# Token mixing kept factored: queries, a head matrix and 64-row mixing matmuls in place of a 256x256 mixing matrix

## The chip, the cores and the metric

The kernel runs on one core of a Trainium2 chip. The metric is the device time of one execution in microseconds (us). The kernel before takes 966.49 us, the median of three runs (966.33 to 966.63).

The engines are called as in the profile: PE multiplies matrices (PEld is its loading of weights), DVE, ACT and POOL work element by element, SP issues DMA transfers. Each engine runs its own stream of instructions in order and waits on semaphores for the others. PE writes only to PSUM; DVE and ACT read PSUM and write SBUF.

## What is computed

There are 8 batches of 3200 tokens with 256 columns. The first half is a gated attention over 64-column z, the second a token mixing:

```python
scores = (1/S) * z @ z.T                     # 3200 x 3200 per batch
x      = u * (np.maximum(scores, 0)**2 @ v)  # 3200 x 256
wq, wk = x @ w_q, x @ w_k                    # 3200 x 64
W_tok  = (1/8) * wq @ wk.T                   # 3200 x 3200
out    = np.maximum(W_tok @ x, 0) @ w_out    # 3200 x 256
```

No 3200 x 3200 matrix is needed for the mixing. With the Gram matrix G = xᵀx (256 x 256), W_tok x is, up to the scale, x Wq Wkᵀ G. The kernel before multiplies Wq Wkᵀ G out to one 256 x 256 matrix per batch and applies it to x. The kernel after keeps it in two factors: q = x Wq with 64 columns, and H = Wkᵀ G with 64 rows.

## The kernel before

**Tiles and steps.** The tokens of a batch on the output side are cut into seven groups (512, 512, 512, 512, 384, 384, 384 wide), those on the summed side into 25 tiles of 128. A (batch, group, tile) triple is one unit. The main loop runs over steps of four units (`GRP = 4`), numbered k, 350 in all. A group is 6.25 steps, a batch 43.75.

**One step.** In step k, `scores(k)` makes two PSUM tiles A and B. Each holds two units, computed by a pair of 64-row matmuls, one on partitions 0 to 63 and one on 64 to 127, in two PSUM banks. `first_stage` empties each tile (relu and a factor) to `g`: A always on DVE, B on ACT where k%5 is 1 or 3 and otherwise on DVE. Then come the functions listed for the start of the step (`early`). `second_stage` squares the `g` of the step before: A's on ACT, B's on POOL. Then `outs(k - 4)` multiplies the squared tiles of four steps earlier (`LAG = 4`) with v into a group's accumulator `acc`; that is 16 matmuls of 256 columns, or 12 in a narrow group. When a group's 25th unit is added, `gate` multiplies `acc` with u on DVE into x. At the end of the step come the functions listed in `late`.

All PSUM tiles come from one pool of four buffers, each two banks: `acc` holds one through a group, and scores and all the mixing tiles share the rest.

**The order is written out by hand.** `at_start` and `at_end` put a function at the start or end of a step. `two(k, first, second)` puts a matmul stage at the end of step k and its copy out of PSUM at the start of step k+1. `end_step(b, gi)` is the step in which the last unit of a group passes `outs`. With E for that step of group 6, a batch's mixing stands as follows: `turn_x` (L274) transposes each group of x by DMA into `xT` at the end of the group's own end step; `gram` (L282) makes G at the end of E+2; `mixw` (L300) multiplies G by the matrix `MT` at the end of E+3, in fp32, with `mixw_out` to `jt` on ACT; `mix` (L318) of group 0 comes at the end of E+4, and those of the other groups four steps after an end step of the next batch, one per group. `mix_out` (L332, ACT, relu) follows at the start of the next step and `proj` (L338) at its end. `proj_out` (L354, ACT, in the last batch DVE) and the output DMA come a step later. In the last batch the mixes stand one per step after E+4, with no scores beside them.

`MT` = Wq Wkᵀ is made once, in steps 8 and 10, by `weights_1` (four fp32 transposes, and the cast of w_out to `wo` on DVE) and `weights_2` (two fp32 matmuls).

**Queues.** SP issues in program order the loads of z and u, the spreading of z, the transposes and the output. POOL issues the loads of v (with a cast), one per batch, nine steps after the batch before begins; group 0 of that batch ends at about the tenth step.

Of the kernel before, what the change touches and what calls it, by code (L numbers as in the profile page):

```python
# [9 lines left out]
FP16 = mybir.dt.float16  # L10
FP32 = mybir.dt.float32
# [5 lines left out]
def kernel(  # L17
# [38 lines left out]
    pg = ctx.enter_context(tc.tile_pool(name="pg", bufs=6))  # L56
    pat = ctx.enter_context(tc.tile_pool(name="pat", bufs=12))
    psml = ctx.enter_context(tc.tile_pool(name="psml", bufs=2))
    prt = ctx.enter_context(tc.tile_pool(name="prt", bufs=2))
    pfo = ctx.enter_context(tc.tile_pool(name="pfo", bufs=3))  # L60
    pps = ctx.enter_context(tc.tile_pool(name="pps", bufs=4, space=bass.MemoryType.PSUM))

    def ps_tile(name, dtype=FP32):
        n = W if dtype == FP32 else 2 * W
        return pps.tile([P, 2, n], dtype, tag="ps", name=name)

    ctx.enter_context(tc.manual_schedule())

    zT, vs, us, xs, xTs, jts = {}, {}, {}, {}, {}, {}


    ZCH = [(0, 4), (4, 7), (11, 7), (18, 7)]
# [72 lines left out]
        us[b, gi] = u_sb  # L145


    ident32 = consts.tile([P, P], FP32, tag="ident32", name="ident32")
    ident = consts.tile([P, P], FP16, tag="ident", name="ident")
    wqk32 = consts.tile([P, 2, 2 * dh], FP32, tag="wqk32", name="wqk32")  # L150
    wT = consts.tile([P, 2, D], FP32, tag="wT", name="wT")
    MT = consts.tile([P, ND, D], FP32, tag="MT", name="MT")
    wo32 = consts.tile([P, 2, D], FP32, tag="wo32", name="wo32")
    wo = consts.tile([P, 2, D], FP16, tag="wo", name="wo")

    def load_weights():
        nc.sync.dma_start(out=wqk32[:, :, 0:dh], in_=moe_w_q.rearrange("(c p) h -> p c h", p=P))
        nc.sync.dma_start(out=wqk32[:, :, dh : 2 * dh], in_=moe_w_k.rearrange("(c p) h -> p c h", p=P))
        nc.sync.dma_start(out=wo32[:], in_=moe_w_out.rearrange("(c p) e -> p c e", p=P))

    def weights_1():
        tp = ps_tile("wtp")
        for which in range(2):
            for ac in range(ND):
                nc.tensor.transpose(
                    tp[0:dh, which, ts(ac, P)], wqk32[:, ac, ds(which * dh, dh)], ident32
                )
        nc.scalar.copy(out=wT[0:dh, :, :], in_=tp[0:dh, :, 0:D])
        nc.vector.tensor_copy(out=wo[:], in_=wo32[:])

    def weights_2():
        mp = ps_tile("mtp")
        for cc in range(ND):
            nc.tensor.matmul(  # L174
                out=mp[:, cc, 0:D],
                lhsT=wT[0:dh, 1, ts(cc, P)],
                rhs=wT[0:dh, 0, :],
                start=True,
                stop=True,
            )  # L180
        nc.scalar.copy(out=MT[:], in_=mp[:, :, 0:D])


    tiles = [(b, gi, ti) for b in range(B) for gi in range(NG) for ti in range(NT)]
# [112 lines left out]
        nc.scalar.copy(out=G[:].rearrange("p a d -> p (a d)"), in_=ps[:, 0, :])  # L297
        return G

    def mixw(b, G):  # L300
        ps = ps_tile("jtp")
        for ac in range(ND):
            for cc in range(ND):
                nc.tensor.matmul(  # L304
                    out=ps[:, ac, 0:D],
                    lhsT=MT[:, cc, ts(ac, P)],
                    rhs=G[:, cc, :],
                    start=(cc == 0),
                    stop=(cc == ND - 1),
                )  # L310
        return ps

    def mixw_out(b, ps):
        jt = psml.tile([P, ND, D], FP16, tag="jt", name="jt")
        nc.scalar.copy(out=jt[:], in_=ps[:, :, 0:D])  # L315
        jts[b] = jt

    def mix(b, gi):  # L318
        gs, gw = starts[gi], widths[gi]
        ps = ps_tile("mx")  # L320
        for db in range(ND):
            for ac in range(ND):
                nc.tensor.matmul(  # L323
                    out=ps[:, db, 0:gw],
                    lhsT=jts[b][:, ac, ds(db * P, P)],
                    rhs=xTs[b][:, gs // P : (gs + gw) // P, ac, :],
                    start=(ac == 0),
                    stop=(ac == ND - 1),
                )
        return ps  # L330

    def mix_out(b, gi, ps):  # L332
        gw = widths[gi]
        rt = prt.tile([P, ND, W], FP16, tag="rt", name="rt")
        nc.scalar.activation(out=rt[:, :, 0:gw], in_=ps[:, :, 0:gw], func=RELU)  # L335
        return rt

    def proj(b, gi, rt):  # L338
        ngb = widths[gi] // P
        ps = ps_tile("fo")  # L340
        for jf in range(0, ngb, 2):
            nj = min(2, ngb - jf)
            for dc in range(ND):
                for j in range(jf, jf + nj):
                    nc.tensor.matmul(  # L345
                        out=ps[:, jf // 2, ds((j - jf) * D, D)],
                        lhsT=rt[:, dc, ts(j, P)],
                        rhs=wo[:, dc, :],
                        start=(dc == 0 and j == jf),
                        stop=(dc == ND - 1 and j == jf + nj - 1),  # L350
                    )
        return ps

    def proj_out(b, gi, ps, on_dve=False):  # L354
        gs, gw = starts[gi], widths[gi]
        fo = pfo.tile([P, 2, W], FP32, tag="fo", name="fo")
        flat_in = ps[:].rearrange("p a w -> p (a w)")[:, 0 : gw // P * D]
        flat_out = fo[:].rearrange("p a w -> p (a w)")[:, 0 : gw // P * D]
        if on_dve:
            nc.vector.tensor_scalar(  # L360
                out=flat_out, in0=flat_in, scalar1=FINAL_SCALE, scalar2=None, op0=AOP.mult
            )
        else:
            nc.scalar.mul(out=flat_out, in_=flat_in, mul=FINAL_SCALE)  # L364
        nc.sync.dma_start(
            out=out[b].rearrange("(n p) d -> p n d", p=P)[:, gs // P : (gs + gw) // P, :],
            in_=flat_out.rearrange("p (n d) -> p n d", d=D),
        )


    late, early = {}, {}

    def at_end(k, fn):
        late.setdefault(k, []).append(fn)
# [4 lines left out]
    def two(k, first, second):  # L379
        def run():  # L380
            r = first()
            at_start(k + 1, lambda: second(r))
        at_end(k, run)

    def end_step(b, gi):
        return ((b * NG + gi) * NT + NT - 1) // GRP + LAG

    for b in range(B):
        for gi in range(NG):
            at_end(end_step(b, gi), lambda b=b, gi=gi: turn_x(b, gi))  # L390
        e = end_step(b, NG - 1)
        keep = {}
        two(e + 2, lambda b=b: gram(b), lambda ps, b=b, keep=keep: keep.update(G=gram_out(b, ps)))
        two(e + 3, lambda b=b, keep=keep: mixw(b, keep["G"]), lambda ps, b=b: mixw_out(b, ps))
        for gi in range(NG):
            if b + 1 < B:
                km = end_step(b, NG - 1) + 4 if gi == 0 else end_step(b + 1, gi - 1) + 4
                kf = km + 1
            else:
                km = e + 4 + gi  # L400
                kf = km + 1
            two(
                km,
                lambda b=b, gi=gi: mix(b, gi),
                lambda ps, b=b, gi=gi, keep=keep: keep.update({gi: mix_out(b, gi, ps)}),
            )
            two(
                kf,
                lambda b=b, gi=gi, keep=keep: proj(b, gi, keep[gi]),
                lambda ps, b=b, gi=gi: proj_out(b, gi, ps, on_dve=(b == B - 1)),  # L410
            )
        k0 = b * NG * NT // GRP
        if b + 1 < B:
            at_start(k0 + 4, lambda b=b: load_z(b + 1))
            for c in range(5):
                at_start(k0 + 8 + 2 * c, lambda b=b, c=c: turn_z(b + 1, c))
            at_start(k0 + 18, lambda b=b: spread_z(b + 1))
            at_start(k0 + 28, lambda b=b: double_z(b + 1))
            at_start(k0 + 9, lambda b=b: load_v(b + 1))
        for gi in range(NG):  # L420
            at_start(max(0, (b * NG + gi) * NT // GRP - 2), lambda b=b, gi=gi: load_u(b, gi))
    at_start(1, load_weights)
    at_end(8, weights_1)
    at_end(10, weights_2)

    make_identity(nc, ident)
    z32, zT2 = load_first()
    make_identity(nc, ident32)
    transpose_first(z32, zT2)

    waiting = []
    k = 0
    while k < NSTEP + LAG or any(x >= k for x in late) or any(x >= k for x in early):
        fresh = []
        if k < NSTEP:
            for i, (p0, sc) in enumerate(scores(k)):
                on_act = i == 1 and k % 5 in (1, 3)
                fresh.append((p0, first_stage(p0, sc, on_act), i == 0))
        for fn in early.pop(k, []):
            fn()  # L440
        for p0, g, on_act in waiting:
            second_stage(p0, g, on_act)
        waiting = fresh
        if 0 <= k - LAG < NSTEP:
            outs(k - LAG)
        for fn in late.pop(k, []):
            fn()
        k += 1
# [30 lines left out]
```

## Time and profile before

| | |
|---|---|
| median of 3 runs | 966.49 us |
| span of the profiled execution, first to last instruction | 966.1 us |
| the same execution's time beyond its span | not given apart; the median lies 0.4 us above the span |
| granted PE clock, mean | 0.995 |
| `mx`, 224 matmuls | 52.4 us busy |
| `jtp`, 64 fp32 records | 15.5 us busy |
| `fo`, 400 matmuls | 53.2 us busy, 13.7 us idle before |
| `rt`, 56 copies on ACT | 52.1 us busy, 42.9 us idle for `mx` |
| transposes to `xT`, 56 | 2.7 / 3.2 / 10.6 us from issue to landing (least, median, most) |

Such a page is read from the whole to the part: first each engine's share of busy time, then the chain, which is followed back from the last instruction and says whose work set the end. A row "L304 PE MATMUL jtp<-G,MT 128*128 128x256 f32 x64 | 15.5, 385 | 0.7 <-ACT G L297 0.7" names the line, the engine, the tile written and those read, the shape, how many, the busy time in us, the mean of one in ns, the idle time of the engine just before these instructions, and what ended most of it. In the timeline a row has its start, its length and the number of instructions merged in it. Matmuls overlap in the pipeline, so the length of a row is more than its claim on PE; what it claims is read from one row's start to the next one's.

### The profile page before, as it was taken

How to read it: one execution, taken by the hardware profiler on the slowest of the kernel's cores; microseconds unless marked ns; L12 is line 12 of the kernel's file. 1: busy time of each engine (PE TensorE's matmuls, PEld its weight loads, DVE VectorE, ACT ScalarE, POOL GpSimd, SP SyncE). 2: the span in 40 equal slices, each digit the busy share in tenths (PEclk: the TensorE clock that was granted, in tenths of full speed). 3: DMA queues.
4: the chain of work that ended last, by engine and by line, in shares of the span. 5: the costliest groups of instructions: out<-in, count | busy, mean ns of one | idle time of the engine just before them, and what ended most of it. 6: DMA issues, size and time to landing. Idle time of an engine off the chain costs nothing.

```text
span 966.1 us, 18206 instructions
## 1 busy us (share of the span) xinstructions
PE 923.2 (96%) x7521; PEld 620.2 (64%) x7521; DVE 699.7 (72%) x762; ACT 541.8 (56%) x626; POOL 611.2 (63%) x373
## 2 busy tenths in 40 slices
PE   5899999999999999999999999999999999999994
PEld 2666676666766667666766666666676666766672
DVE  5897958777596776877677775886858777576833
ACT  4455546566465665566556564756646566466542
POOL 5677766667576675666666665666756767566620
PEclk8999999999999999999999999999999999999999
DMA  9723337444573267342484442852628522131313
GB/s 204 99 44 89 73 60 140 93 92 119 67 132 89 74 127 124 73 111 63 111 121 96 96 114 55 124 124 63 135 46 141 126 60 88 43 88 50 92 50 136
DMA packets 204691, 92.51 MB, mean 96 GB/s; under 512 B 127104, under 2 KB 204160, under 8 KB 204608
## 3 DMA queue, kind: packets, MB, share of 16 engines
q1 hardware_dynamic: 178832, 78.24, 34.9%
q0 software_dynamic: 25776, 13.11, 10.5%
q8 instruction: 59, 0.97, 0.4%
q14 instruction: 24, 0.20, 0.1%
HBM read 59.38 MB, written 26.21 MB: 89 GB/s over the span
## 4 chain that ended last, share of the span: by engine, by line
PE 82%; DVE 8%; issue 5%; ACT 4%; DMA 1%; SPq 0%; DVEq 0%; ACTq 0%
PE acc L248 50%; PE sc L197 16%; DVE g L221 7%; PE fo L345 5%; PE xtx L286 5%; PE mx L323 4%; ACT rt L335 3%; PE jtp L304 1%; DMA z<-in_z_dram 1%; ACT g L217 0%; DVE x_sb L268 0%; SPq L79 0%; DVE zs L118 0%; PE mtp L174 0%; DVE fo L360 0%
## 5 line engine op out<-in xcount | busy, mean ns | idle before, releaser
L233 POOL TENSOR_TENSOR at<-g 128x1024 f16<-128x1024 f32 (+2 forms) x354 | 595.5, 1694 | 316.2 <-DVE g L221 289.7
L221 DVE TENSOR_SCALAR g<-sc 128x1024 f32<-128x1024 f32 (+2 forms) x564 | 596.5, 1097 | 220.1 <-PE sc L197 216.5
L248 PE MATMUL acc<-v_sb,at 128*128 128x256 f16 x5000 | 610.6, 274 | 2.6 <-DVE g L221 2.6
L248 PEld LDWEIGHTS <-at 128*128 128x128 f16 x5000 | 461.6, 98 | 176.0 <-issue 114.8
L231 ACT ACTIVATE at<-g 128x1024 f16<-128x1024 f32 (+2 forms) x354 | 326.4, 952 | 23.8 <-DVE g L221 23.3
L217 ACT ACTIVATE g<-sc 128x1024 f32<-128x1024 f32 (+2 forms) x144 | 130.8, 911 | 295.0 <-PE sc L197 290.1
L197 PE MATMUL sc<-zT 64*128 64x512 f16 (+1 forms) x1400 | 204.6, 361 | 11.8 <-DVE g L221 8.4
L197 PEld LDWEIGHTS <-zT 64*128 64x128 f16 x1400 | 46.2, 94 | 107.7 <-issue 103.5
L335 ACT ACTIVATE rt<-mx 128x1024 f16<-128x1024 f32 (+1 forms) x56 | 52.1, 930 | 42.9 <-PE mx L323 42.9
L268 DVE TENSOR_TENSOR x_sb<-acc,u_sb 128x512 f16<-128x512 f32 x112 | 65.2, 623 | 12.5 <-PE acc L248 12.3
L345 PE MATMUL fo<-wo,rt 128*128 128x256 f16 x400 | 53.2, 274 | 13.7 <-ACT rt L335 13.5
L345 PEld LDWEIGHTS <-rt 128*128 128x128 f16 x400 | 36.6, 98 | 27.4 <-ACT rt L335 23.5
L323 PE MATMUL mx<-xT_sb,jt 128*128 128x512 f16 (+1 forms) x224 | 52.4, 357 | 0.7 <-ACT jt L315 0.7
L364 ACT ACTIVATE fo<-fo 128x1024 f32<-128x1024 f32 (+1 forms) x49 | 45.5, 929 | 6.1 <-PE fo L345 6.1
L286 PE MATMUL xtx<-x_sb 128*128 128x256 f16 x400 | 45.0, 273 | 0.0
L286 PEld LDWEIGHTS <-x_sb 128*128 128x128 f16 x400 | 39.2, 98 | 4.5
L323 PEld LDWEIGHTS <-jt 128*128 128x128 f16 x224 | 21.7, 98 | 13.2 <-ACT jt L315 1.1
L360 DVE TENSOR_SCALAR fo<-fo 128x1024 f32<-128x1024 f32 (+1 forms) x7 | 7.8, 1110 | 20.8 <-PE fo L345 20.8
L297 ACT COPY G<-xtx 128x512 f32<-128x512 f32 x8 | 4.7, 583 | 30.0 <-PE xtx L286 30.0
L119 DVE STREAM_TRANSPOSE zst<-zs 128x320 f16<-128x320 f16 x35 | 17.9, 511 | 1.2
L304 PE MATMUL jtp<-G,MT 128*128 128x256 f32 x64 | 15.5, 385 | 0.7 <-ACT G L297 0.7
L118 DVE CAST zs<-z 128x320 f16<-128x320 f32 x35 | 16.0, 456 | 0.0
(23 smaller groups left out, 53.2 us busy)
## 6 DMA issues: line engine op xcount, KB each, us to landing
u_sb<-in_u_dram SPq DMA_DIRECT2D x32, 512.0 KB, 4.9
out_dram<-fo SPq DMA_DIRECT2D x32, 512.0 KB, 3.2
v_sb<-in_v_dram POOLq DMA_DIRECT2D x7, 1600.0 KB, 15.8
u_sb<-in_u_dram SPq DMA_DIRECT2D x24, 384.0 KB, 3.9
out_dram<-fo SPq DMA_DIRECT2D x24, 384.0 KB, 2.7
z<-in_z_dram SPq DMA_DIRECT2D x7, 800.0 KB, 6.1
zT<-zst SPq DMA_DIRECT2D x56, 50.0 KB, 2.4
zT<-zT SPq DMA_DIRECT2D x7, 400.0 KB, 4.9
```

What stands on the lines that cost most here:

```text
L197: nc.tensor.matmul(out=sc[:, h, 0:gw], lhsT=zT[b][half : half + dqk, ts(ti, P)], rhs=zT[b][half : half + dqk, ds(gs, gw)], start=True, sto ...
L217: nc.scalar.activation(out=g[:, hs, 0:w], in_=sc[:, hs, 0:w], func=RELU, scale=GSCALE)
L221: nc.vector.tensor_scalar(out=g[:, hs, 0:w], in0=sc[:, hs, 0:w], scalar1=0.0, scalar2=GSCALE, op0=AOP.max, op1=AOP.mult,)
L231: nc.scalar.square(out=at[:, hs, 0:w], in_=g[:, hs, 0:w])
L233: nc.gpsimd.tensor_mul(out=at[:, hs, 0:w], in0=g[:, hs, 0:w], in1=g[:, hs, 0:w])
L248: nc.tensor.matmul(out=acc[:, j // 2, ds((j % 2) * D, D)], lhsT=at[:, h, ts(j, P)], rhs=vs[b][:, ti, :], start=(ti == 0 and j % 2 == 0), s ...
L268: nc.vector.tensor_mul(out=xs[b][:, n0 + j : n0 + j + nj, :].rearrange("p n d -> p (n d)"), in0=acc[:, j // 2, 0 : nj * D], in1=u_sb[:, j ...
L286: nc.tensor.matmul(out=ps[:, 0, ds(cc * D, D)], lhsT=xs[b][:, ti, ds(cc * P, P)], rhs=xs[b][:, ti, :], start=(ti == 0 and cc == 0), stop=( ...
L323: nc.tensor.matmul(out=ps[:, db, 0:gw], lhsT=jts[b][:, ac, ds(db * P, P)], rhs=xTs[b][:, gs // P : (gs + gw) // P, ac, :], start=(ac == 0) ...
L335: nc.scalar.activation(out=rt[:, :, 0:gw], in_=ps[:, :, 0:gw], func=RELU)
L345: nc.tensor.matmul(out=ps[:, jf // 2, ds((j - jf) * D, D)], lhsT=rt[:, dc, ts(j, P)], rhs=wo[:, dc, :], start=(dc == 0 and j == jf), stop= ...
L364: nc.scalar.mul(out=flat_out, in_=flat_in, mul=FINAL_SCALE)
```

## The change

The matrix `MT` and its making (`weights_1`, `weights_2`, the fp32 identity) go. Instead Wq (fp16) and Wk (fp32) are held with their 64 columns written twice side by side, by four DVE casts in `cast_weights` at the start of step 10; the cast of `wo` moves there too.

Per group, `queries` multiplies the doubled Wq with `xT`: two matmuls at the end of the step three after the group's end step. The result, qᵀ on partitions 0 to 63 and again on 64 to 127, is copied to fp16 by ACT at the start of the next step (`queries_out`), where it waits in a pool of ten buffers. Per batch, `heads` multiplies the doubled Wk with G: two fp32 matmuls where `mixw` had four, at the end of E+3, behind the last group's queries; `heads_out` copies 128x256 to fp16.

`mix` now takes two matmuls of 64 rows in place of four of 128. One works on partitions 0 to 63, the other on 64 to 127, each with 128 of the 256 output columns. `mix_step` puts it one step later than before and at another place in the step: behind the step's scores, in front of `outs`. `mix_out` is the first of that step's start functions, and `proj` comes at the end of the same step, so `proj` stays in the step in which it was.

```diff
+    pq = ctx.enter_context(tc.tile_pool(name="pq", bufs=10))
-    def weights_1():
...
-    def weights_2():
...
+    def cast_weights():
+        for half in range(2):
+            nc.vector.tensor_copy(out=wq2[:, :, half, :], in_=wq32[:])
+            nc.vector.tensor_copy(out=wk2[:, :, half, :], in_=wk32[:])
         nc.vector.tensor_copy(out=wo[:], in_=wo32[:])
...
-    def mixw(b, G):
-        ps = ps_tile("jtp")
...
+    def heads(b, G):
+        ps = ps_tile("hd")
+        for cc in range(ND):
+            nc.tensor.matmul(
+                out=ps[:, 0, 0:D],
+                lhsT=wk2[:, cc, :, :].rearrange("p t h -> p (t h)"),
+                rhs=G[:, cc, :],
...
+    def heads_out(b, ps):
+        hs = psml.tile([P, D], FP16, tag="hs", name="hs")
+        nc.scalar.copy(out=hs[:], in_=ps[:, 0, 0:D])
...
+    def queries(b, gi):
+        gs, gw = starts[gi], widths[gi]
+        ps = ps_tile("qq")
         for ac in range(ND):
+            nc.tensor.matmul(
+                out=ps[:, 0, 0:gw],
+                lhsT=wq2[:, ac, :, :].rearrange("p t h -> p (t h)"),
+                rhs=xTs[b][:, gs // P : (gs + gw) // P, ac, :],
...
+    def queries_out(b, gi, ps):
+        gw = widths[gi]
+        qt = pq.tile([P, W], FP16, tag="qt", name="qt")
+        nc.scalar.copy(out=qt[:, 0:gw], in_=ps[:, 0, 0:gw])
...
     def mix(b, gi):
...
         for db in range(ND):
-            for ac in range(ND):
-                nc.tensor.matmul(
-                    out=ps[:, db, 0:gw],
-                    lhsT=jts[b][:, ac, ds(db * P, P)],
-                    rhs=xTs[b][:, gs // P : (gs + gw) // P, ac, :],
...
+            half = db * dh
+            nc.tensor.matmul(
+                out=ps[:, db, 0:gw],
+                lhsT=hss[b][half : half + dh, ds(db * P, P)],
+                rhs=qt[half : half + dh, 0:gw],
...
+    def mix_step(k, b, gi):
+        def run():
+            ps = mix(b, gi)
+            kept = {}
+            early.setdefault(k, []).insert(0, lambda: kept.update(rt=mix_out(b, gi, ps)))
+            two(
+                k,
+                lambda: proj(b, gi, kept["rt"]),
+                lambda ps: proj_out(b, gi, ps, on_dve=(b == B - 1)),
+            )
+
+        beside[k] = run
...
-        two(e + 3, lambda b=b, keep=keep: mixw(b, keep["G"]), lambda ps, b=b: mixw_out(b, ps))
+        for gi in range(NG):
+            two(
+                end_step(b, gi) + 3,
+                lambda b=b, gi=gi: queries(b, gi),
+                lambda ps, b=b, gi=gi: queries_out(b, gi, ps),
+            )
+        two(e + 3, lambda b=b, keep=keep: heads(b, keep["G"]), lambda ps, b=b: heads_out(b, ps))
...
-                km = end_step(b, NG - 1) + 4 if gi == 0 else end_step(b + 1, gi - 1) + 4
-                kf = km + 1
+                km = e + 5 if gi == 0 else end_step(b + 1, gi - 1) + 5
...
-    at_end(8, weights_1)
-    at_end(10, weights_2)
+    at_start(10, cast_weights)
...
                 fresh.append((p0, first_stage(p0, sc, on_act), i == 0))
+        if k in beside:
+            beside.pop(k)()
         for fn in early.pop(k, []):
```

More of the change, by code (lines that the diff above doesn't have):

```diff
@@ L67 @@
     ctx.enter_context(tc.manual_schedule())
-    zT, vs, us, xs, xTs, jts = {}, {}, {}, {}, {}, {}
+    zT, vs, us, xs, xTs, hss, qts = {}, {}, {}, {}, {}, {}, {}
     ZCH = [(0, 4), (4, 7), (11, 7), (18, 7)]
@@ L145, in load_u @@
         us[b, gi] = u_sb
-    ident32 = consts.tile([P, P], FP32, tag="ident32", name="ident32")
     ident = consts.tile([P, P], FP16, tag="ident", name="ident")
-    wqk32 = consts.tile([P, 2, 2 * dh], FP32, tag="wqk32", name="wqk32")
-    wT = consts.tile([P, 2, D], FP32, tag="wT", name="wT")
-    MT = consts.tile([P, ND, D], FP32, tag="MT", name="MT")
+    wq32 = consts.tile([P, ND, dh], FP32, tag="wq32", name="wq32")
+    wk32 = consts.tile([P, ND, dh], FP32, tag="wk32", name="wk32")
+    wq2 = consts.tile([P, ND, 2, dh], FP16, tag="wq2", name="wq2")
+    wk2 = consts.tile([P, ND, 2, dh], FP32, tag="wk2", name="wk2")
     wo32 = consts.tile([P, 2, D], FP32, tag="wo32", name="wo32")
@@ L156, in load_weights @@
     def load_weights():
-        nc.sync.dma_start(out=wqk32[:, :, 0:dh], in_=moe_w_q.rearrange("(c p) h -> p c h", p=P))
-        nc.sync.dma_start(out=wqk32[:, :, dh : 2 * dh], in_=moe_w_k.rearrange("(c p) h -> p c h", p=P))
+        nc.sync.dma_start(out=wq32[:], in_=moe_w_q.rearrange("(c p) h -> p c h", p=P))
+        nc.sync.dma_start(out=wk32[:], in_=moe_w_k.rearrange("(c p) h -> p c h", p=P))
         nc.sync.dma_start(out=wo32[:], in_=moe_w_out.rearrange("(c p) e -> p c e", p=P))
-    def weights_1():
-        tp = ps_tile("wtp")
-        for which in range(2):
-            for ac in range(ND):
[L165 to L169, printed above, removed]
-    def weights_2():
-        mp = ps_tile("mtp")
-        for cc in range(ND):
-            nc.tensor.matmul(
[L175 to L181, printed above, removed]
+    def cast_weights():
+        for half in range(2):
+            nc.vector.tensor_copy(out=wq2[:, :, half, :], in_=wq32[:])
+            nc.vector.tensor_copy(out=wk2[:, :, half, :], in_=wk32[:])
+        nc.vector.tensor_copy(out=wo[:], in_=wo32[:])
     tiles = [(b, gi, ti) for b in range(B) for gi in range(NG) for ti in range(NT)]
@@ L298, in gram_out @@
         return G
-    def mixw(b, G):
-        ps = ps_tile("jtp")
-        for ac in range(ND):
[L303 to L310, printed above, removed]
-        return ps
[L313 to L316, printed above, removed]
+    def heads(b, G):
[5 more added lines that the diff above has]
+                rhs=G[:, cc, :],
+                start=(cc == 0),
+                stop=(cc == ND - 1),
+            )
+        return ps
@@ new lines, in heads_out @@
+    def heads_out(b, ps):
+        hs = psml.tile([P, D], FP16, tag="hs", name="hs")
+        nc.scalar.copy(out=hs[:], in_=ps[:, 0, 0:D])
+        hss[b] = hs
+    def queries(b, gi):
+        gs, gw = starts[gi], widths[gi]
+        ps = ps_tile("qq")
+        for ac in range(ND):
+            nc.tensor.matmul(
+                out=ps[:, 0, 0:gw],
+                lhsT=wq2[:, ac, :, :].rearrange("p t h -> p (t h)"),
+                rhs=xTs[b][:, gs // P : (gs + gw) // P, ac, :],
+                start=(ac == 0),
+                stop=(ac == ND - 1),
+            )
+        return ps
@@ L318, in mix @@
+    def queries_out(b, gi, ps):
+        gw = widths[gi]
+        qt = pq.tile([P, W], FP16, tag="qt", name="qt")
+        nc.scalar.copy(out=qt[:, 0:gw], in_=ps[:, 0, 0:gw])
+        qts[b, gi] = qt
     def mix(b, gi):
-        gs, gw = starts[gi], widths[gi]
+        gw = widths[gi]
         ps = ps_tile("mx")
+        qt = qts.pop((b, gi))
         for db in range(ND):
-            for ac in range(ND):
-                nc.tensor.matmul(
-                    out=ps[:, db, 0:gw],
-                    lhsT=jts[b][:, ac, ds(db * P, P)],
-                    rhs=xTs[b][:, gs // P : (gs + gw) // P, ac, :],
-                    start=(ac == 0),
-                    stop=(ac == ND - 1),
-                )
+            half = db * dh
[3 more added lines that the diff above has]
+                rhs=qt[half : half + dh, 0:gw],
+                start=True,
+                stop=True,
+            )
@@ L368, in proj_out @@
         )
-    late, early = {}, {}
+    late, early, beside = {}, {}, {}
     def at_end(k, fn):
@@ L383, in two @@
         at_end(k, run)
+    def mix_step(k, b, gi):
[7 more added lines that the diff above has]
+                lambda ps: proj_out(b, gi, ps, on_dve=(b == B - 1)),
+            )
+        beside[k] = run
     def end_step(b, gi):
@@ L393 @@
         two(e + 2, lambda b=b: gram(b), lambda ps, b=b, keep=keep: keep.update(G=gram_out(b, ps)))
-        two(e + 3, lambda b=b, keep=keep: mixw(b, keep["G"]), lambda ps, b=b: mixw_out(b, ps))
+        for gi in range(NG):
[3 more added lines that the diff above has]
+                lambda ps, b=b, gi=gi: queries_out(b, gi, ps),
+            )
+        two(e + 3, lambda b=b, keep=keep: heads(b, keep["G"]), lambda ps, b=b: heads_out(b, ps))
         for gi in range(NG):
             if b + 1 < B:
-                km = end_step(b, NG - 1) + 4 if gi == 0 else end_step(b + 1, gi - 1) + 4
-                kf = km + 1
-            else:
[L400 to L411, printed above, removed]
+                km = e + 5 if gi == 0 else end_step(b + 1, gi - 1) + 5
+            else:
+                km = e + 5 + gi
+            mix_step(km, b, gi)
         k0 = b * NG * NT // GRP
@@ L422 @@
     at_start(1, load_weights)
-    at_end(8, weights_1)
-    at_end(10, weights_2)
+    at_start(10, cast_weights)
     make_identity(nc, ident)
     z32, zT2 = load_first()
-    make_identity(nc, ident32)
     transpose_first(z32, zT2)
@@ L432 @@
     k = 0
-    while k < NSTEP + LAG or any(x >= k for x in late) or any(x >= k for x in early):
+    while k < NSTEP + LAG or any(x >= k for x in late) or any(x >= k for x in (*early, *beside)):
         fresh = []
```

## The prediction, made before the changed kernel ran

> **What bounds the kernel now.** I read the page's engine shares, then the chain of waits, then groups by shape, then the timeline around one mixing step, then the transposes one by one.
>
> ```profile
> span 966.1 us, 18206 instructions
> PE 923.2 (96%) x7521; PEld 620.2 (64%) x7521; DVE 699.7 (72%) x762; ACT 541.8 (56%) x626; POOL 611.2 (63%) x373
> PE 82%; DVE 8%; issue 5%; ACT 4%; DMA 1%; SPq 0%; DVEq 0%; ACTq 0%
> ...
> L304 PE MATMUL jtp<-G,MT 128*128 128x256 f32 x64 | 15.5, 385 | 0.7 <-ACT G L297 0.7
> ```
>
> PE is busy 96% of the span and 82% of the chain, so columns streamed through PE are time. The timeline around two mixing steps of the fifth batch (start, length) gives their price:
>
> ```profile
> 503.95 0.61 PE L197 MATMUL sc<-zT 64*128 64x512 f16 x4
> 504.49 1.92 PE L248 MATMUL acc<-v_sb,at 128*128 128x256 f16 x16
> 506.24 1.03 PE L323 MATMUL mx<-xT_sb,jt 128*128 128x512 f16 x4
> 507.20 0.61 PE L197 MATMUL sc<-zT 64*128 64x512 f16 x4
> 507.74 1.92 PE L248 MATMUL acc<-v_sb,at 128*128 128x256 f16 x16
> 509.50 1.04 PE L345 MATMUL fo<-wo,rt 128*128 128x256 f16 x8
> ...
> 523.64 0.60 PE L197 MATMUL sc<-zT 64*128 64x512 f16 x4
> 524.17 1.92 PE L248 MATMUL acc<-v_sb,at 128*128 128x256 f16 x16
> 524.37 1.02 ACT L217 ACTIVATE g<-sc 128x1024 f32<-128x1024 f32 x1 [3.55 <-PE sc L197]
> 525.28 1.02 ACT L335 ACTIVATE rt<-mx 128x1024 f16<-128x1024 f32 x1
> 526.36 1.05 PE L345 MATMUL fo<-wo,rt 128*128 128x256 f16 x8 [0.26 <-ACT rt L335]
> ```
>
> Read start to start. Four mx take 0.96 us: 4 x 0.216 plus 0.096 for going back to 64-row work. Four sc (two pairs) take 0.54: a pair costs 0.216, like one full matmul. Sixteen acc take 1.75 to fo. A plain 512-wide step takes 2.39, a 384-wide one 1.845. From 523.64 on, ACT has g before rt (the steps with k%5 of 1 or 3) and fo starts 2.19 after the acc instead of 1.75: 0.43 lost.
>
> Whatever PE must wait for counts too. The queries read xT three steps after the transpose is issued; today a group's mix reads it most of a batch later. The transposes, with one at 498.95 as an example, and then two places where DVE holds the PSUM or itself:
>
> ```profile
> L276 SPq DMA_TRANSPOSE xT_sb<-x_sb x56: 1211/1252/2824, 43.3 to 934.0; - x56
> DMA to landing us min/median/max: 2.7/3.2/10.6
> ...
> 498.95 2.52 SPq L276 DMA_TRANSPOSE xT_sb<-x_sb  x1
> ...
> 33.70 3.10 DVE L169 CAST wo<-wo 128x512 f16<-128x512 f32 x1
> ...
> 137.54 0.61 PE L197 MATMUL sc<-zT 64*128 64x512 f16 x4
> 138.04 1.23 DVE L221 TENSOR_SCALAR g<-sc 128x1024 f32<-128x1024 f32 x1 [1.77 <-PE sc L197]
> ```
>
> **The change part by part.** Below, E is the step in which a group's gate ends.
>
> *Mixing.* Per group four streams become two (queries) and one pair (mix): 3 instead of 4 units, 0.216 at 512 columns, 0.162 at 384 (four mx there: 903.98 to 904.73). 32 x 0.216 + 24 x 0.162 = 10.8 us. The last batch, alone at the end with fo waiting for rt, saves three units of four per group on the path but has paid queries earlier and changes row mode seven times: about the same 1.35. PE thins out there from some 67% busy to 59% (1.4 of 2.44 us per group, was 2.05 of 3.09); 945 to 950 us is 54% busy at clock 1.00, so I take no drop of the clock, at worst 7 x 1.1 = 7.7 us of streams at half speed.
>
> *Heads.* Eight fp32 records per batch run from 135.71 to 137.54, 0.216 each; four remain: 8 x 0.864 = 6.9.
>
> *Cover of rt.* In the 24 or so mixing steps where ACT has g first, fo is held by ACT at 2.19. The new pair now stands before the acc, inside that wait: it costs nothing there, 24 x 0.19 = 4.6. If ACT were late by more than that, the cover is gone and this term is 0.
>
> *Start.* wtp, mtp, their copies and ident32 go. PE lost 4.3 us around 33 to 42 us, 1.9 of it because the wo cast held DVE for 3.10 us while POOL worked. The cast moves to step 10 with four 128x128 casts beside it (about 0.2 each from 128x320 in 0.32), ahead of the gate, which then comes late. I take 0.5 gained; ends -2 and +3.
> [...]
>
> *ACT.* 56 query copies (0.58 as G, about 0.49 at 384) are 30 us more on a 56% engine. They fall in step E+4, before rt (E+5) and fo (E+6), so no step has two extras, save at a batch's end, where the copy of H is 0.2 shorter. Squares behind them have LAG of four steps. I take 0; at most 3 lost, as ACT idles 42.9 us for mx before rt.
>
> *POOL, SP and DVE queues.* POOL loses only ident32, before its first multiply. SP has the same issues in the same order. DVE gains the four casts alone.
>
> *Loss 1: waiting for xT.* Queries would start about 0.1 us before step E+4 does today. Comparing this with each transpose's landing (all 56): group 0 of batches 2 to 7 lands 6.7, 5.9, 5.3, 10.6, 7.9 and 5.6 us after issue, while the next batch's 1600 KB of v arrives (15.8 us), and has 5.7, 5.0, 6.2, 5.0, 5.7, 5.0 until that start. Late by 1.05, 1.0, 0, 5.7, 2.3, 0.7, and one group 3 by 0.6: 11.3 us, all on PE, with the next scores queued behind. A long gap also costs clock. The stages of the start show it (length, PE busy; the clock stands behind the five engines):
>
> ```profile
> 15.30:18.70 3.40, 1.40 (x10) 0.31 (x6) 3.40 (x4) 3.13 (x4) 3.40 (x2) 0.86 1.33 190
> 18.70:22.00 3.30, 3.30 (x17) 2.20 (x16) 3.04 (x3) 2.45 (x3) 3.30 (x3) 0.50 1.13 225
> ```
>
> After 3.4 us at 41% busy the clock is 0.50, and the two steps after lose 2.6 us. The 5.7 wait could do that, hardly a shorter one: I add 1.5, so 12.8. Bounds: 3 if the 10.6 and 7.9 do not recur, 21 if three such do.
> [...]
>
> *Loss 2: PSUM.* In the built program 36 of the mx tiles take the buffer of the B scores of the step before. DVE empties it 2.32 us after the acc starts (1.84 at 384); mx wants it at 2.39 (1.845). So no wait at 512, 0.07 at 384, but 0.45 to 0.76 where scores are already 512 wide and acc still 384 (groups 5). The B scores behind queries wait 0.44 in three steps and 0.28 in one: 1.6. Of mx, outside ACT's cover 0.07 four times and 0.45 twice: 1.2; beyond the cover of 0.22, 0.54 and 0.23 twice each and 0.15 once: 1.7. Off go 0.75 of present waits of scores in the same places: 3.8; bounds 1 and 7. Behind a waiting mx stand the step's acc. Its other inputs, qt and hs, are a step old or more: no time.
>
> *Loss 3: a batch's end.* There queries, heads, acc and scores hold four of four buffers. In two steps (51 and 226) scores B get the buffer of scores A of the same step: B waits 0.5 + 1.23 + 0.06 after A starts instead of 0.216, 1.57 more, by DVE's g at 138.04 for sc at 137.54: 3.1 us; bounds 0 and 4.
>
> *Sum.* 10.8 + 6.9 + 4.6 + 0.5 = 22.8 gained, 12.8 + 3.8 + 3.1 = 19.7 lost: 3.1 off the execution's span of 966.1. The median 966.49 lies 0.4 above that span; 966.5 - 3.1 = 963.4, say 963.
>
> **The rivals.**
> *The transposes hold PE much longer.* One mechanism, at group 0 of seven batches: every landing like the 10.6 makes 5.0 to 5.7 late each, 7 x 5.3 = 37, and 7 x 2.6 = 18 of clock, instead of 12.8: 963 + 42 = 1005 at the worst; two more like the 10.6 give 963 + 11 = 974. It decides from 16 us of waiting on: 2.3 per batch, a landing of about 8 us. For it: all landings under a v load were over 5. Against: the median of all is 3.2, and only two passed 7. Chance 0.24.
> *The transposes land in time*, as group 0 of the last batch (3.9): then 963 - 10 = 953 (3 of 12.8 left), less if DVE, too, keeps up. Chance 0.17.
> *Nothing measurable* (within 0.2%, 1.9 us, about what this kernel's measurement resolves): PSUM waits at their bound of 7, or the 4.6 under ACT's wait not gained: 966 to 968. Chance 0.19.
>
> **How the numbers follow.** The forecast, 963, with its own range 957 to 964.5, has 0.40. With the rivals the range goes down to 953 less 1 for a better start and up to 974, the longer wait with two more bad landings; beyond lie about half of that rival and a third of the one of landing in time, 0.18. Faster 0.40 + 0.17 = 0.57, same 0.19, slower 0.24.
>
> **What would show it.** In the profile after: the heads group with 32 records and about 7.7 us; mx with 112 records in pairs 0.003 apart, behind sc; fo's idle for rt, 13.5 with 7.5 of it in the last batch's tail, nearly gone before that tail; PE idle before qq released by the DMA, some 11 us, nearly all in group 0 of batches 2 to 7, with a clock below 1 behind the longest; a sc waiting about 1.5 us on DVE at steps 51 and 226; ACT near 570 us busy. Wrong, if PE waits for qt or hs on ACT, if mx waits on DVE in most groups by more than 0.3, or if DVE's new casts stretch past 4 us.

## The result and the profile after

The changed kernel takes 973.78 us (median of four runs, 972.54 to 975.10) against 966.41 us before on the same chip: a ratio of 1.0072, 95% interval 1.0058 to 1.0086. It is 0.7% slower. The kernel was forecast to be faster: the forecast was 963; 973.8 lies just inside the range's upper end of 974, on the side that had a chance of 0.24.

The profiled execution took 972.54 us. The head of its page, with the shares of the chain:

```profile
span 970.8 us, 18193 instructions
PE 916.2 (94%) x7481; PEld 612.7 (63%) x7481; DVE 700.6 (72%) x766; ACT 565.5 (58%) x680; POOL 610.0 (63%) x371
...
PE 76%; DVE 10%; DMA 6%; issue 4%; ACT 1%; POOL 1%; DVEq 0%; SPq 0%; ACTq 0%
```

PE does 7 us less work than before (923.2) in a span that is 4.7 us longer. DMA's share of the chain went from 1% to 6%: something waits for a transfer. The groups of the mixing (busy, mean ns | idle before and its cause), and then PE's waits (in total, times, longest):

```profile
L349 PE MATMUL fo<-wo,rt 128*128 128x256 f16 x400 | 55.7, 282 | 7.8 <-ACT rt L339 7.8
L306 PE MATMUL qq<-xT_sb,wq 128*128 128x512 f16 (+1 forms) x112 | 31.3, 361 | 12.9 <-DMA xT_sb<-x_sb 12.9
L327 PE MATMUL mx<-qt,hs 64*128 64x512 f16 (+1 forms) x112 | 20.9, 365 | 1.9 <-DVE g L206 1.4 <-ACT hs L299 0.5
L288 PE MATMUL hd<-G,wk 128*128 128x256 f32 x32 | 8.3, 382 | 0.3 <-ACT G L282 0.3
```

```profile
PE qq L306 <- DMA xT_sb<-x_sb: 12.9, 8, 6.1
PE sc L182 <- DVE g L206: 9.3, 16, 1.4
PE fo L349 <- ACT rt L339: 7.8, 8, 1.2
...
PE sc L182 <- DVE x_sb L253: 3.8, 2, 3.5
```

The transposes themselves, from issue to landing, are as they were but for the longest (10.6 before):

```profile
L261 SPq DMA_TRANSPOSE xT_sb<-x_sb x56: 1211/1260/2968, 44.0 to 940.0; - x56
...
DMA to landing us min/median/max: 2.7/3.1/11.1
```

The mixing itself became what the change says. The timeline of one mixing step where ACT has g first, the counterpart of the one at 523.64 before:

```profile
533.18 0.61 PE L182 MATMUL sc<-zT 64*128 64x512 f16 x4
533.70 0.39 PE L327 MATMUL mx<-qt,hs 64*128 64x512 f16 x2
533.91 1.02 ACT L202 ACTIVATE g<-sc 128x1024 f32<-128x1024 f32 x1 [1.47 <-PE sc L182]
534.02 1.92 PE L233 MATMUL acc<-v_sb,at 128*128 128x256 f16 x16
534.83 1.02 ACT L339 ACTIVATE rt<-mx 128x1024 f16<-128x1024 f32 x1
535.90 1.05 PE L349 MATMUL fo<-wo,rt 128*128 128x256 f16 x8
```

From sc to fo it is 2.72 us, as before (523.64 to 526.36), although the pair now stands in between: in such a step it costs nothing.

So where did the time go? I compare the starts of the same steps in the two traces. The profiled execution of before had a span of 966.1; after is 4.7 longer. By stage:

| stage | forecast by the prediction's terms | measured | what differs |
|---|---|---|---|
| up to step 14 | 0.0 (0.5 gained, group 0's first queries 0.54 paid) | +1.6 | casts held by POOL |
| steps 14 to 346 | +1.6 | +4.4 | waits for xT 14.2 instead of 11.3, clock 3.0 instead of 1.5, the rest 1.6 better |
| last steps and tail | -4.6 | -1.3 | half clock, about 3.0 |
| sum | -3.0 | +4.7 | 7.7 |

Three of these readings, in the trace of after. First the start, DVE and POOL beside PE (start, length):

```profile
34.50 7.57 POOL L218 TENSOR_TENSOR at<-g 128x1024 f16<-128x1024 f32 x4
...
38.92 1.39 DVE L164 CAST wq<-wq 128x128 f16<-128x128 f32 x1
40.23 1.93 DVE L165 COPY wk<-wk 128x128 f32<-128x128 f32 x1
42.08 0.21 DVE L164 CAST wq<-wq 128x128 f16<-128x128 f32 x1
...
42.68 1.28 DVE L253 TENSOR_TENSOR x_sb<-acc,u_sb 128x512 f16<-128x512 f32 x2
...
44.01 0.61 PE L182 MATMUL sc<-zT 64*128 64x512 f16 x4 [3.53 <-DVE x_sb L253]
44.55 3.48 PE L233 MATMUL acc<-v_sb,at 128*128 128x256 f16 x16
```

A cast of 0.21 us takes 1.39 and its neighbour 1.93 while POOL multiplies end to end until 42.07; from then on they take 0.21. The gate stands behind them, the next scores wait 3.53 us for it, and the acc after this gap take 3.48 us instead of 1.92: half clock (0.59 granted from 44.0 to 48.0).

Second, the longest wait for a transpose, in batch 5, and the granted clock there, after another wait (of 2.55 us from 273.6 on), and in the tail. The windows give length, then busy time of PE, PEld, DVE, ACT and POOL, then the clock (0.50 is half clock), and last the DMA engines' share and GB/s:

```profile
504.62 1.92 PE L233 MATMUL acc<-v_sb,at 128*128 128x256 f16 x16
512.59 1.04 PE L306 MATMUL qq<-xT_sb,wq 128*128 128x512 f16 x2 [6.05 <-DMA xT_sb<-x_sb]
513.56 1.03 PE L182 MATMUL sc<-zT 64*128 64x512 f16 x4
514.52 2.50 PE L233 MATMUL acc<-v_sb,at 128*128 128x256 f16 x16
```

```profile
277.00:280.50 3.50, 3.50 (x20) 2.15 (x16) 1.97 (x3) 2.45 (x3) 1.67 (x2) 0.54 0.00 0
...
509.00:515.50 6.50, 2.91 (x11) 1.00 (x12) 1.22 (x2) 1.54 (x2) 0.00 (x0) 0.50 0.83 144
...
948.00:956.00 8.00, 4.27 (x32) 2.55 (x33) 3.67 (x3) 3.21 (x4) 0.00 (x0) 1.00 0.39 131
956.00:966.00 10.00, 7.10 (x32) 3.31 (x30) 3.14 (x3) 2.43 (x3) 0.00 (x0) 0.50 0.50 171
```

Third, the same tail as a timeline: eight fo take 1.05 us, and from 955.84 on 1.71, at half clock.

```profile
953.29 1.05 PE L349 MATMUL fo<-wo,rt 128*128 128x256 f16 x8 [1.18 <-ACT rt L339]
...
955.84 1.71 PE L349 MATMUL fo<-wo,rt 128*128 128x256 f16 x8 [1.18 <-ACT rt L339]
```

### The profile page after: what moved, and what is told of

It reads as the page before. It is cut to its first block, busy times and chain, and to the rows that moved or that the text cites. A ratio compares the mean times of both kernels' runs of the same rounds, so it can differ in the third digit from the quotient of the medians.

```text
span 970.8 us, 18193 instructions
## 1 busy us (share of the span) xinstructions
PE 916.2 (94%) x7481; PEld 612.7 (63%) x7481; DVE 700.6 (72%) x766; ACT 565.5 (58%) x680; POOL 610.0 (63%) x371
## 3 DMA queue, kind: packets, MB, share of 16 engines
q0 software_dynamic: 25776, 13.11, 10.4%
## 4 chain that ended last, share of the span: by engine, by line
PE 76%; DVE 10%; DMA 6%; issue 4%; ACT 1%; POOL 1%; DVEq 0%; SPq 0%; ACTq 0%
PE acc L233 47%; PE sc L182 15%; DVE g L206 9%; DMA xT_sb<-x_sb 6%; PE fo L349 5%; PE xtx L271 4%; PE qq L306 2%; PE mx L327 2%; POOL at L218 1%; ACT rt L339 1%; PE hd L288 1%; DMA z<-in_z_dram 1%; DVE x_sb L253 1%; DVE wk L165 0%; PE ztp L97 0%
## 5 line engine op out<-in xcount | busy, mean ns | idle before, releaser
L182 PE MATMUL sc<-zT 64*128 64x512 f16 (+1 forms) x1400 | 205.9, 364 | 15.9 <-DVE g L206 9.3
L253 DVE TENSOR_TENSOR x_sb<-acc,u_sb 128x512 f16<-128x512 f32 x112 | 65.2, 623 | 12.5 <-PE acc L233 12.3
L349 PE MATMUL fo<-wo,rt 128*128 128x256 f16 x400 | 55.7, 282 | 7.8 <-ACT rt L339 7.8
L318 ACT CAST qt<-qq 128x512 f16<-128x512 f32 (+1 forms) x56 | 30.1, 538 | 35.2 <-PE qq L306 34.8
L306 PE MATMUL qq<-xT_sb,wq 128*128 128x512 f16 (+1 forms) x112 | 31.3, 361 | 12.9 <-DMA xT_sb<-x_sb 12.9
L327 PE MATMUL mx<-qt,hs 64*128 64x512 f16 (+1 forms) x112 | 20.9, 365 | 1.9 <-DVE g L206 1.4
L306 PEld LDWEIGHTS <-wq 128*128 128x128 f16 x112 | 10.3, 98 | 16.2 <-DMA xT_sb<-x_sb 15.1
```

The source lines that it names most:

```text
L182: nc.tensor.matmul(out=sc[:, h, 0:gw], lhsT=zT[b][half : half + dqk, ts(ti, P)], rhs=zT[b][half : half + dqk, ds(gs, gw)], start=True, sto ...
L253: nc.vector.tensor_mul(out=xs[b][:, n0 + j : n0 + j + nj, :].rearrange("p n d -> p (n d)"), in0=acc[:, j // 2, 0 : nj * D], in1=u_sb[:, j ...
L306: nc.tensor.matmul(out=ps[:, 0, 0:gw], lhsT=wq2[:, ac, :, :].rearrange("p t h -> p (t h)"), rhs=xTs[b][:, gs // P : (gs + gw) // P, ac, :] ...
L349: nc.tensor.matmul(out=ps[:, jf // 2, ds((j - jf) * D, D)], lhsT=rt[:, dc, ts(j, P)], rhs=wo[:, dc, :], start=(dc == 0 and j == jf), stop= ...
```

## The experiments

Ratios are to the kernel before, run on the same chip (966.6 to 967.4 us; a difference between two experiments can hold that much of the chips). Each edit is to the changed kernel unless another is named.

### Group 0's queries four steps later

```diff
-                end_step(b, gi) + 3,
+                end_step(b, gi) + (7 if gi == 0 else 3),
```

> Only the queries of group 0 move, from three to seven steps after the group's end step. Theory (PE stands waiting for the transposes of group 0, and each longer wait also costs a stretch at half clock): the waits of group 0, 13.4 us in the profile after, and some 3 us of half clock behind them go: 957 us against 973.8, no drop of the clock in the middle of the run. Rival (the waits only stand in front of another limit, DVE or PSUM, that takes their place): at least half comes back elsewhere, 965 us or more.

962.03 us (961.93 to 963.74), ratio 0.9957 (0.9941 to 0.9972): 11.8 us less than the changed kernel, and now faster than before. Group 0's transposes still land 6.2 to 11.6 us after issue in batches 2 to 7, but nothing asks for them so soon:

```profile
PE qq L306 <- DMA xT_sb<-x_sb: 0.7, 2, 0.5
```

The waits and the clock behind them are thus worth about 12 us. The time falls between the theory's 957 and the rival's 965, and of the missing 5 us the trace shows two parts: new waits of PE behind the moved queries, 3.6 us in all (scores wait for g 11.1 us instead of 9.3 and for the gate 5.1 instead of 3.8, mx for g 1.9 instead of 1.4), and, in the profiled execution (963.74), a tail 3.3 us longer than that of the changed kernel, since the half clock begins earlier there (0.69 granted from 930 to 946, 0.50 from 946 to 956; the changed kernel has 1.00 until 956).

### The load of v five steps later

```diff
-            at_start(k0 + 9, lambda b=b: load_v(b + 1))
+            at_start(k0 + 14, lambda b=b: load_v(b + 1))
```

> The changed kernel, with each batch's load of the next v issued five steps later (step 14 of a batch in place of 9), nothing else. Theory: the transposes of group 0 land late because the v load runs beside them, so its queries then wait for nothing (landings of about 3 us), and the load runs beside group 1's transposes, whose landings grow to 5 us or more: the waits of queries on the transposes, 14 us in the changed kernel, turn up in group 1 (some 12 us later in each batch) in place of group 0, and the time stays within 968 to 978. Rival: something else at a batch's start (the loads of z and its spreading) delays them, and group 0's queries still wait as long, group 1's not.

974.39 us (972.22 to 975.69), ratio 1.0070 (1.0046 to 1.0094). The time is in the expected band, the reason is not. Group 0's transposes in batches 2 to 7 land 3.1 to 4.2 us after issue, where they took 6.1 to 11.1, so the load beside them was the cause. But the waits did not move to group 1 (3.0 to 4.6 us there, in time for its queries): they are gone, down to 1.0 us on PE's weight loads. My premise was off: the load issued at 625.03 lands 16.8 us later, at 641.85, and so fits between the transposes of group 0, at 618.59, and of group 1, at 641.89; in four other batches only its last 0.5 to 3.4 us run beside group 1's. In their place DVE is late. The timeline behind one load, and PE's wait for DVE's g, which was 9.3:

```profile
625.03 1.58 POOL L106 DMA_DIRECT2D v_sb<-in_v_dram  x1
...
626.63 5.59 POOL L218 TENSOR_TENSOR at<-g 128x1024 f16<-128x1024 f32 x3
...
627.51 4.91 DVE L119 CAST zs<-z 128x320 f16<-128x320 f32 x1
```

```profile
PE sc L182 <- DVE g L206: 15.8, 19, 3.2
```

Issuing the load keeps POOL 1.58 us. It then does three multiplies end to end, and a cast of z that takes 0.32 us alone takes 4.91, until 0.2 us after POOL's last multiply is done. Five such casts (4.91, 3.46, 2.61, 4.91, 3.46) raise the busy time of all 35 from 16.3 to 33.1 us, and the steps that hold them and those just behind are longer than in the changed kernel by 15.8 us in all, half clock behind two of them included (0.89 granted from 158 to 174, 0.91 from 624 to 638). Step by step the waits and the clock that went were worth 16.5 us, and between steps 14 and 346 the two kernels take 872.0 and 872.6. The gain was paid back by a second mechanism that I had not foreseen here, though it is the one that spoiled the start.

### All queries later

```diff
-                end_step(b, gi) + 3,
+                end_step(b, gi) + (7 if b + 1 < B else 3),
```

> The queries of all groups but the last batch's move to seven steps after the end step; with that no two scores of one step share a PSUM buffer any more. Theory: beyond the first of these runs, the remaining 0.8 us of waits for transposes and the two waits of 1.6 us at steps 51 and 226 go: 953 us. Rival (those two waits are hidden, since what follows them waits for ACT anyway): as the first run, 956 to 958.

969.84 us (966.87 to 970.57), ratio 1.0022 (1.0010 to 1.0035). Both theories missed by more than ten. Seven steps after a group's end is the step in which the next group's gate stands. Two acc hold PSUM buffers there, queries take the buffer that the gate empties, and the scores behind wait for the gate in 12 places (0.5 to 1.6 us each), besides the 3.5 us of the start, and elsewhere for g or for the queries' copy on ACT:

```profile
PE sc L182 <- DVE x_sb L253: 12.6, 13, 3.5
```

In the changed kernel this was 3.8 us in two places. Between steps 14 and 346 this kernel takes 7.9 us more than the one with group 0's queries late alone. A later place for the queries is good for group 0, which has nearly all the late transposes, and bad for the others.

### The casts on ACT, alone and with group 0's queries late

```diff
-            nc.vector.tensor_copy(out=wq2[:, :, half, :], in_=wq32[:])
-            nc.vector.tensor_copy(out=wk2[:, :, half, :], in_=wk32[:])
-        nc.vector.tensor_copy(out=wo[:], in_=wo32[:])
+            nc.scalar.copy(out=wq2[:, :, half, :], in_=wq32[:])
+            nc.scalar.copy(out=wk2[:, :, half, :], in_=wk32[:])
+        nc.scalar.copy(out=wo[:], in_=wo32[:])
```

> The five casts of the weights run on ACT instead of DVE, at the same place. Theory (DVE's casts were shut out by POOL multiplies for 1.4 and 1.9 us, the gate came late, PE stood 3.8 us and then ran 3.4 us at half clock): some 4.5 us less, 969 us, with no gap of PE near 40 us. Rival (the gate's place alone makes the gap): less than 1 us gained.

975.53 us, but from 966.76 to 979.02: inconclusive. The profiled execution, the shortest of them, has no 3.5-us wait for the gate any more, but 14.5 us of waits for transposes; its times are spread over 12 us, more than the term in question is worth. So I repeated the edit on top of the kernel with group 0's queries late, where they are gone:

> The queries of group 0 late, and the five weight casts on ACT. With the transposes out of the way, the casts can be judged. Theory (the gap of 3.8 us near 40 us and the half clock behind it come from DVE's casts standing behind POOL): 4.5 us less than the kernel with group 0's queries late alone, 957.5. Rival (the casts on ACT are what made the run with casts alone slow, 975.5): 962 or more.

956.74 us (956.16 to 959.83), ratio 0.9896 (0.9878 to 0.9913): 5.3 less than without the edit, as expected. From step 10 to step 14 PE needs 9.9 us, with the casts on DVE 14.9, and the kernel before needs 13.5 there. PE's wait for the gate, first with the casts on DVE and then on ACT, both with group 0's queries late:

```profile
PE sc L182 <- DVE x_sb L253: 5.1, 3, 3.5
...
PE sc L182 <- DVE x_sb L253: 1.6, 2, 0.8
```

The casts on DVE beside POOL cost 5 us. The start was to gain 0.5; with the casts on ACT it gains 3.5 (9.9 against 13.5).

### The tail kept warm, and the tail filled

The first kernel puts matmuls of no use into fo's PSUM tile ahead of fo in the last batch, while PE waits for rt; fo overwrites them.

```diff
         ps = ps_tile("fo")
+        if b == B - 1:
+            for _ in range(2 * ngb):
+                nc.tensor.matmul(
+                    out=ps[:, 0, 0:D],
+                    lhsT=xs[b][:, 0, 0:P],
+                    rhs=xs[b][:, 0, :],
...
```

> In the last batch, useless matmuls (six or eight of 256 columns, overwritten afterwards) fill PE's wait for rt ahead of each fo. Theory (the sparser tail of the changed kernel drops the clock to half from its fourth group on): the clock stays at 1 to the end of the mixing and the time falls by 3 us to 971. Rival (the tail is bound by ACT and the clock does not matter there): no gain, or slower by the 0.65 to 0.87 us per group that the added work takes.

970.59 us (967.76 to 974.82), ratio 1.0041 (1.0023 to 1.0059): 3.2 less than the changed kernel, by doing more. The times of the two kernels overlap (the changed one's begin at 972.54), so the trace has to say where the gain lies: the clock stays whole to the end (its mean over the run is 0.989, that of the changed kernel 0.985), and from step 346 to the end it takes 44.3 us where the changed kernel takes 47.3. That is the 3.0 us of half clock read from the tail.

A better use of the gaps is work that is needed. On top of the kernel with group 0's queries late and the casts on ACT, the last batch's projections go one step later, so that the next group's pair stands between a relu and the projection that waits for it:

```diff
             two(
-                k,
+                k if b + 1 < B else k + 1,
                 lambda: proj(b, gi, kept["rt"]),
```

> As the version with group 0's queries late and the casts on ACT (956.7), and in the last batch alone each projection one step later, so that the next group's pair of mixing matmuls stands between the relu and the projection that needs it. Theory: the tail's ten us that the version with all three parts showed come from this edit alone, and the seven that it lost come from moving group 6: 946.5, range 945 to 949, with the clock whole up to the last projections and no mx waiting 1.2 us or more on DVE. Rival: the tail was only short because group 6's queries had left the step of the heads there, or the loss of that version is not group 6's: 951 or more.

948.88 us (947.77 to 949.75), ratio 0.9804 (0.9789 to 0.9819), in the expected range at its upper end: 18 us faster than the kernel before. From the Gram matrix to the end it takes 24.1 us where it took 32.1. The timeline of its tail:

```profile
933.59 1.05 PE L349 MATMUL fo<-wo,rt 128*128 128x256 f16 x8
934.57 0.39 PE L327 MATMUL mx<-qt,hs 64*128 64x512 f16 x2
934.89 1.05 PE L349 MATMUL fo<-wo,rt 128*128 128x256 f16 x8
```

In these rows no fo waits, and eight of them take 1.05 us; in the whole tail two fo wait, 0.9 and 0.2 us, and the clock is whole until the last of them is done (1.00 from 927 to 939, and the last six take 0.83 us like the six before).

### The mix back at the end of a step

Made on the kernel with group 0's queries late: the pair again at the end of the step before, as in the kernel before, except in the last batch.

```diff
-        beside[k] = run
+        if b + 1 < B:
+            at_end(k - 1, run)
+        else:
+            beside[k] = run
```

> The queries of group 0 late, and the mix of all batches but the last at the end of the step before, ahead of the next scores, instead of behind them. Theory (behind the scores the pair lies under the wait of fo for rt in the steps where ACT has g first, 4.6 us, against about 3 us of waits for a PSUM buffer that this place costs): 1.5 us more than with group 0's queries late alone, 963.5. Rival (the place behind the scores costs more in PSUM waits than it hides): 960 or less.

972.81 us (971.57 to 974.30), ratio 1.0055 (1.0038 to 1.0071), 10.8 more than with the pair behind the scores; in the traces 7.5 of it lie between steps 16 and 316, and 2.2 in the start, which the edit does not touch. Theory and rival both had the place worth little or less than nothing. The waits show why it is not:

```profile
PE fo L349 <- ACT rt L339: 13.5, 27, 1.2
PE sc L182 <- DVE g L206: 13.2, 25, 1.4
```

The wait of fo for rt is back (13.5 us as before the change; 7.8 with the pair behind the scores, nearly all of it in the tail), and the PSUM waits that the end of the step should have saved only changed hands: mx waits for DVE 0 us instead of 1.9, the scores 13.2 instead of 11.1. So the cover that I put at 4.6 is worth 5.7 by fo's wait, and the place as a whole 7.5; what makes the rest of it was not tried.

### Group 6's queries a step later, alone and with the rest

This was to undo the waits of the scores in steps 51 and 226, also on the kernel with group 0's queries late. The timeline of after at step 51, with scores B waiting for scores A of the same step:

```profile
140.94 0.39 PE L182 MATMUL sc<-zT 64*128 64x512 f16 x2
141.44 1.22 DVE L206 TENSOR_SCALAR g<-sc 128x1024 f32<-128x1024 f32 x1 [1.22 <-PE sc L182]
...
142.72 0.39 PE L182 MATMUL sc<-zT 64*128 64x512 f16 x2 [1.39 <-DVE g L206]
```

```diff
-                end_step(b, gi) + (7 if gi == 0 else 3),
+                end_step(b, gi) + (7 if gi == 0 else 4 if gi == 6 and b + 1 < B else 3),
```

> The queries of group 0 late, and those of group 6 one step later, so that they no longer stand in one step with the heads and no two scores of one step share a buffer. Theory: the two waits of 1.6 us at steps 51 and 226 go, 959 us. Rival (the extra tile's place in another step costs the same): 961.5 to 962.5.

969.86 us (968.14 to 972.34), ratio 1.0026 (1.0016 to 1.0036): 7.8 more, not 3 less. Steps 51 and 226 gain 1.24 each, as foreseen. But the step after holds queries, scores A and B, mx and acc, five tiles in four buffers, and mx takes the buffer of its own step's scores A, in all seven batches (1.1 to 1.6 us each, 9.9 in all):

```profile
143.04 0.60 PE L182 MATMUL sc<-zT 64*128 64x512 f16 x4
144.82 0.39 PE L327 MATMUL mx<-qt,hs 64*128 64x512 f16 x2 [1.18 <-DVE g L206]
145.15 1.92 PE L233 MATMUL acc<-v_sb,at 128*128 128x256 f16 x16
```

The version with all parts (group 0's queries late, casts on ACT, tail filled, group 6 moved):

> Group 0's queries late, group 6's one step later, casts on ACT, and in the last batch the mix of the next group ahead of the projection of this one. Theory: 4.5 us from the start, 3.2 from the PSUM buffers, and in the tail PE no longer stands waiting for rt (about 1.2 us in each of seven groups) nor loses its clock (3 us): 943 us. Rival (the tail's clock drops in any case, as PE has little work there): 948 or more.

956.24 us (955.71 to 958.28), ratio 0.9888 (0.9873 to 0.9903). It missed by 13, and it has both the tail's gain (24.1 us from the Gram matrix to the end) and group 6's loss (mx waits 11.3 us for DVE, 1.9 where group 6's queries were not moved). Without group 6's move the same kernel is the one of 948.88 above: the move alone costs 7.4 here, 7.8 there.

## Why the prediction was wrong

The mechanisms were all named; what failed is the size of its losses. *Start* (a gain of 0.5), *Loss 1* with its clock (12.8), the clock of the tail (0) and the base were each put too low, by 1.5, 4.4, 3.0 and 1.4 us, and that turned a gain of 3 us into a loss of 7. One by one:

**Right: the sum in the running steps.** Mixing, heads and cover were to save, and the scores' collisions and PSUM to cost, what they did: between steps 14 and 346 the traces differ by +4.4 us. Take from that the waits for xT (14.2, start to start), the clock behind them (3.0) and the two collisions (1.57 each, as priced), and -15.9 remains; the prediction's terms give -14.3 there. The heads saved their 0.864 a batch, the scores of steps 51 and 226 waited as said. *Cover* was mis-sized: 5.7 by fo's wait for rt, 7.5 with all that the place brings, instead of 4.6. ACT at 565.5 us and fo's idle before the tail came out as written.

**Right in kind, short in size: "Loss 1".** The waits fell in group 0 of batches 2 to 7, by the v load that two runs have now shown to be the cause of the late landings and of the lost time: 14.2 us against 11.3. The single landings were not those of the trace before (group 0 of batch 3 came at 7.4 instead of 5.9 us, of batch 7 at 7.3 instead of 5.6, of batch 6 at 6.2 instead of 7.9), so that the two sums lie this near is in part luck. "I add 1.5" for the clock was half of it: behind a wait of 2.55 us, which I had thought too short for it, half clock cost some 1.5 too. The rival that the transposes hold PE much longer is the side on which the result fell, but it is not what happened: 14.2 stays under the 16 from which it was to decide, and its step of 2.3 per batch was passed in three batches (2.55, 6.21 and 2.45).

**Wrong: "Start".** "I take 0.5 gained" became 1.0 lost; two of the five casts met POOL's multiplies. I had priced four of them at about 0.2 each, after the casts of z: 28 of 35 take 0.31 to 0.32 us in the trace of before, the other seven 0.78 to 1.17. What I took was the common case over the whole run; at this place POOL works end to end for 7.57 us, and the row of the same place stood among my own, the wo cast at 3.10. The casts that took 1.39 and 1.93 us each ended about 0.1 us behind one of POOL's multiplies of 1.89 us. The one of 4.91 us in a later run shows that the length of one multiply is no bound: it ended 0.2 us behind the last of three, 5.59 us together. My own sign of failure, DVE's new casts past 4 us together, is met: 1.39 + 1.93 + 0.21 + 0.21 + 0.41 = 4.15. By the pair of runs with group 0's queries late, the casts off DVE are worth 5.3.

**Wrong: "I take no drop of the clock"** in the tail. The row I took it from (945 to 950, 54% busy, clock 1.00) was one thin stretch of 5 us between two busier ones, 64% and 72%:

```profile
940.00:945.00 5.00, 3.21 (x19) 1.81 (x18) 0.06 (x1) 1.61 (x2) 0.00 (x0) 1.00 0.00 0
945.00:950.00 5.00, 2.68 (x16) 1.25 (x14) 2.39 (x2) 2.05 (x2) 0.00 (x0) 1.00 0.30 105
950.00:955.00 5.00, 3.61 (x24) 2.18 (x24) 2.02 (x2) 1.11 (x2) 0.00 (x0) 1.00 0.62 209
```

It could not show what a whole tail at that share does. The tail of after keeps the clock whole at 53% busy for 8 us, and then runs at 0.50 to the end: 3.0 us of the 7.7 that I had named as the worst. No wait of PE in this tail is over 1.2 us (1.18 the longest), so short gaps alone were no safeguard.

**Wrong: the base.** "The median 966.49 lies 0.4 above that span" mixed two executions. In every run here for which both are given, the time is 1.7 to 1.9 us above its own span. By that, and this is an estimate, the profiled execution of before took about 967.9, some 1.4 more than the median. I subtracted from the execution and counted from the median, which made 1.4 us of gain out of nothing.

These account for it: 1.6 (start), 2.8 (xT and clock, less the better rest), 3.3 (tail), 1.4 (base) make 9.1 of the 10.4 between 963.4 and 973.8; the median run lies 1.2 above the profiled one, and I have no trace of it.

The plan of the change was sound. With group 0's queries and the casts mended it is worth 10.7 us (967.44 to 956.74, on one chip), and with the filled tail 18. That last step is more than a mended fault: it also takes away waits of fo for rt that the kernel before has (7.5 us in its tail), and the kernel before was not run with a filled tail, or with its own cast on ACT. So the 18 us can't be set beside the 22.8 that the prediction summed up as gains.

## What to carry to other kernels

Before a consumer is moved towards its producer, list every landing of the transfer between them, and what runs beside the late ones: here one group in seven needed another place, and moving all seven gave back two thirds of what moving the one had gained (7.8 of 11.8 us). Count the PSUM tiles alive in each step against the pool before moving a stage by a step; the fifth tile in four buffers cost more than the wait that the move was to remove (9.9 us against 2.5). Put short copies where POOL's work doesn't hold them up, here on ACT, and look at POOL at that very place, not at the average.

## What the runs showed of the hardware that I had not expected

- A PE wait of 2.55 us was followed by 3.4 us at half clock (0.54 in the window 277.0 to 280.5), another of 2.45 us at 743.6 by none (1.00 from 743.6 to 750.0).
- PE work broken by gaps of at most 1.2 us every 2.5 us (53% busy) ran at full clock for some 8 us and then at 0.50 until the end of the kernel. In the other traces with the same code in the tail the drop came 3.9 to 11.4 us behind the Gram matrix (with group 0's queries late the clock is 0.69 from 930 to 946; with the casts on ACT besides, eight fo take 1.89 us from 942.93 on), where it took 11.7 in this one; why it comes when it does is not shown.
- A DVE cast of 0.32 us stayed open for 4.91 us while POOL did three multiplies end to end. Yet the one of 38.92 in the changed kernel ended after 1.39 us, 1.8 us before POOL's stretch did. What decides whether a cast gets in between two multiplies is not shown.
- Group 0's transposes of batches 2 to 7 land 3.1 to 4.2 us after issue, and 5.3 to 11.6 us beside a 1600-KB load that POOL issues. The times of kernels whose PE waits for them were spread by 2.6 to 12.3 us, those of the others by 1.8 to 4.2; that the landings make this spread was not tried.
